# Spectral filter and FFN layers on one core: layer 1 folds along d by a half turn, with normalised rows and a constant table

## The chip, the cores and the metric

The kernel runs on 1 core of one Trainium2 chip. The metric is the time of one execution in device microseconds; lower is better. The engines are PE (TensorE matmul; PEld is its weight load), DVE (VectorE), ACT (ScalarE), POOL (GpSimd) and SP (SyncE, which here only issues DMAs).

## The reference

```python
def _A_ref(x, w_r, w_i):              # spectral filter over (S, D) = (2048, 448)
    X = jnp.fft.rfft2(x.astype(jnp.float32), axes=(-2, -1))
    X = X * (w_r + 1j * w_i)          # weights (2048, 225)
    return jnp.fft.irfft2(X, s=(S, D), axes=(-2, -1)).astype(jnp.bfloat16)

def _B_ref(x, w1, b1, w2, b2):        # FFN 448 -> 1792 -> 448
    h = jnp.einsum("bsd,df->bsf", x, w1) + b1
    r = jnp.where(h > 0, h, 0)
    return jnp.einsum("bsf,fd->bsd", r * r, w2) + b2

x = A_x                               # (1, 2048, 448) bf16
x = x + _A_ref(_layernorm(x), A_w_r, A_w_i)
x = x + _B_ref(_layernorm(x), B_w1, B_b1, B_w2, B_b2)
x = x + _A_ref(_layernorm(x), A_w_r, A_w_i)   # the same weights again
x = x + _B_ref(_layernorm(x), B_w1, B_b1, B_w2, B_b2)
```

## The kernel before

Two layers, each a spectral filter and an FFN. The 2048 rows lie in 16 tiles of 128 (row = 16 p + t), and stay on the chip. The Fourier transforms are matrix products.

A spectral stage of layer 1 runs through these steps; the names are those of the planner's tags.

- **A1** (`first_A`, one unit for each tile t): the transform of 128 points over the partitions. A tile of x is folded along d first: the table turns the sum and the difference of two halves of a row into even and odd parts. The folding happens on PE: the tile `xin` is multiplied by the table twice, and the second half of its row, mirrored, by the table with its signs. The mirrored half is a copy, `xr`, that lies in `VT` (`XR` items). The layer norm enters through the table: `Fs` is the constant table `FA_sb` (128x256) times the tile's 1/std, made anew for each tile, and a fifth matmul on `m2` (minus twice the mean) takes the mean away. So a tile has 5 matmuls of 256 columns; the last tile does them in two halves. The statistics come from DVE (`bn_stats`, `bn_aggr`), for tiles 1, 3 and 5 from two passes of ACT (`act_stats`); the root is ACT's, the reciprocal DVE's. The result is evacuated into `XA`.
- **TD** (`stage_TD`): the transform along d, 64 matmuls on `TD_sb`, evacuated into `arena`.
- **B**: 66 matmuls on `G_sb`, in four row and column groups of PE, again into `arena`.
- **W** (`stage_W`): 16 products on DVE with the filter weights `Wt`, into `wide`. `Wt` is filled by four gathers of 0.92 MB (indirect DMAs, issued by POOL, which need the index load `ix`). Each product reads from all four, so the first one waits for all.
- **Bi**: 256 matmuls on `H_sb`, in 8 blocks of 32, evacuated into `VT`.
- **TI, AI**: the inverse transform along d and over the partitions; TI needs all of `VT`. Then follow the second layer norm, the FFN (`W1_sb` and `W2_sb`, in the profile `W_sb`), and at the end of layer 1 the first transform of layer 2 (A2).

Every instruction is recorded by helpers (`mm`, `evac`, `scaled`, `act` and others) as an item. A planner gave the order of items on each engine, and this order is written out as tables of numbers, one for each engine (`ORDER`). At build time the items are placed in that order, waits on semaphores are derived from reads and writes, and fillers (matmuls on `ones`, line 1367) go into holes of PE that the planner's model sees, at the start and at two or three places later. DMAs go through the queues of SP, ACT (five of the loads of x) and POOL (the gathers); each queue works in its order, and a DMA behind a wait of its engine's sequencer is issued after that wait.

Some loads are gated by an `after`: the two halves of `H_sb` wait for the 1/std of tiles 10 and 12, `W1_sb` for the evacuation of Bi's block 1.

Of the kernel before, what the change touches and what calls it, by code (L numbers as in the profile page):

```python
# [150 lines left out]
1265 1270 1275 1236 1242 1280 1283 1286 1289 1292""",  # L151
    "act": """
# [11 lines left out]
1226 1035 1172 1184 1177 1174 1179 1182 1253 1246 1248 1251 1256 1261 1268 1278 1266 1263 1271 1258 1273 1276""",  # L164
    "dve": """
# [22 lines left out]
1039 1284 1281 1243 1287 1290 1293""",  # L188
    "pool": """
16 24 25 17 41 23 27 29 81 26 28 22 30 104 21 31 20 32 143 146 18 19""",  # L190
    "sp": """
3 5 6 8 9 11 13 15 33 34 35 150 151 152 153 154 155 156 157 158 159 233 234 235 236 281 301 319 322 321 339 357 375
# [1266 lines left out]
```

## Time and profile before

| | |
|---|---|
| median of 3 runs | 256.01 us (255.53 to 256.25) |
| the profiled execution, its own time | 255.97 us |
| its span | 254.2 us |
| PE busy | 246.8 us (97%), 2462 matmuls |
| DVE busy | 193.3 us (76%) |
| ACT busy | 166.4 us (65%) |
| POOL busy | 12.5 us (5%), all in the first 19 us |
| granted PE clock | 1.0 |

Times of the rows below are microseconds from the start of the span, and the 1.8 us between span and time are the same in every comparison made here. A row has start, length, engine, line, operation, out<-in, the shape, and in brackets how long the engine stood idle ahead of it and what released it. Instructions overlap a little, so a row of several is a better price for one than a row of one. A busy PE need not be at its peak.

### The profile page before, as it was taken

How to read it: one execution, taken by the hardware profiler on the slowest of the kernel's cores; microseconds unless marked ns; L12 is line 12 of the kernel's file. 1: busy time of each engine (PE TensorE's matmuls, PEld its weight loads, DVE VectorE, ACT ScalarE, POOL GpSimd, SP SyncE). 2: the span in 40 equal slices, each digit the busy share in tenths (PEclk: the TensorE clock that was granted, in tenths of full speed). 3: DMA queues.
4: the chain of work that ended last, by engine and by line, in shares of the span. 5: the costliest groups of instructions: out<-in, count | busy, mean ns of one | idle time of the engine just before them, and what ended most of it. 6: DMA issues, size and time to landing. Idle time of an engine off the chain costs nothing.

```text
span 254.2 us, 6150 instructions
## 1 busy us (share of the span) xinstructions
PE 246.8 (97%) x2462; PEld 154.2 (61%) x2462; DVE 193.3 (76%) x628; ACT 166.4 (65%) x362; POOL 12.5 (5%) x26
## 2 busy tenths in 40 slices
...
GB/s 198 367 330 383 56 148 327 96 41 45 36 41 44 0 4 0 41 43 3 0 3 1 3 3 3 3 44 43 59 81 23 0 3 41 38 87 64 3 0 146
DMA packets 24080, 18.10 MB, mean 71 GB/s; under 512 B 16082, under 2 KB 22706, under 8 KB 24052
## 3 DMA queue, kind: packets, MB, share of 16 engines
...
q10 hardware_dynamic: 720, 0.80, 1.1%
q8 instruction: 19, 0.31, 0.5%
q14 instruction: 9, 0.07, 0.1%
...
## 4 chain that ended last, share of the span: by engine, by line
PE 74%; DVE 10%; ACT 8%; DMA 4%; POOL 1%; issue 1%; SPq 0%; POOLq 0%; DVEq 0%
PE ps L724 74%; ACT arena L749 5%; DVE wide L778 3%; ACT VT L749 2%; DMA FA_sb<-c_FA 2%; DMA wide<-wide 2%; DVE st L854 1%; ACT wide L749 1%; DVE Fs L761 1%; DVE VT L750 1%; DVE XA L750 1%; DVE x_sb L1217 1%; POOL VT L750 1%; DVE arena L750 1%; PE ps L1367 0%
## 5 line engine op out<-in xcount | busy, mean ns | idle before, releaser
L724 PE MATMUL ps<-wide,W_sb 64*128 64x512 bf16 (+1 forms) x770 | 90.0, 346 | 0.2 <-DMA wide<-wide 0.2
L724 PE MATMUL ps<-W_sb,arena 128*128 128x448 bf16 (+3 forms) x476 | 86.8, 342 | 0.0
L724 PEld LDWEIGHTS ps<-wide,W_sb 64*128 64x128 bf16 (+1 forms) x770 | 51.4, 95 | 36.3 <-issue 0.7
L743 ACT ACTIVATE arena<-ps,b1col 128x512 bf16<-128x512 f32 x84 | 52.0, 691 | 29.2 <-PE ps L724 28.9
L724 PEld LDWEIGHTS ps<-W_sb,arena 128*128 128x128 bf16 x476 | 45.5, 98 | 38.1 <-ACT arena L743 0.4
L778 DVE TENSOR_TENSOR arena<-arena 128x512 bf16<-128x512 bf16 (+1 forms) x140 | 44.0, 362 | 29.8 <-ACT arena L743 29.8
L1095 ACT ACTIVATE VT<-x_sb 128x448 bf16<-128x448 bf16 x28 | 16.1, 582 | 13.2 <-DVE x_sb L1071 13.2
L749 ACT ACTIVATE arena<-ps 128x896 bf16<-128x896 f32 (+1 forms) x27 | 20.6, 852 | 3.1 <-PE ps L724 3.1
L743 ACT ACTIVATE mv<-mv,epst 128x1 f32<-128x1 f32 (+1 forms) x45 | 12.8, 297 | 12.0 <-DVE mv L855 8.4
L743 ACT ACTIVATE arena<-ps 128x256 bf16<-128x256 f32 x56 | 17.9, 400 | 0.9 <-PE ps L724 0.7
L778 DVE TENSOR_TENSOR wide<-arena,Wt 128x896 bf16<-128x896 bf16 x32 | 17.8, 620 | 0.4 <-ACT arena L749 0.4
L749 ACT ACTIVATE XA<-ps 128x512 bf16<-128x512 f32 (+1 forms) x28 | 15.3, 595 | 3.2 <-PE ps L724 3.2
L1217 DVE SCALAR_TENSOR_TENSOR x_sb<-ps,mv,xin 128x448 bf16<-128x448 f32 (+2 forms) x13 | 8.0, 644 | 11.7 <-PE ps L724 11.5
L724 PE MATMUL ps<-wide,VT 64*128 64x512 bf16 x42 | 15.8, 376 | 0.0
L749 ACT ACTIVATE wide<-ps 128x896 bf16<-128x896 f32 (+3 forms) x20 | 14.1, 762 | 2.4 <-PE ps L724 2.3
L724 PE MATMUL ps<-H_sb,wide 64*128 64x128 bf16 x512 | 15.5, 216 | 0.1
L724 PEld LDWEIGHTS ps<-H_sb,wide 64*128 64x128 bf16 x512 | 14.4, 94 | 2.0 <-ACT arena L749 1.3
L749 ACT ACTIVATE VT<-ps 128x512 bf16<-128x512 f32 (+1 forms) x16 | 12.2, 885 | 0.0
L1367 PE MATMUL ps<-ones 128*128 128x512 bf16 (+2 forms) x32 | 10.4, 450 | 1.7 <-POOL ones L791 1.0
L760 ACT ACTIVATE wide<-x_sb,rstd 128x448 bf16<-128x448 bf16 x12 | 7.8, 665 | 6.3 <-DVE mv L787 6.0
L750 DVE CAST arena<-ps 128x448 bf16<-128x448 f32 (+1 forms) x11 | 8.8, 831 | 3.1 <-PE ps L724 3.1
L1071 DVE SCALAR_TENSOR_TENSOR x_sb<-ps,mv,xin 128x448 bf16<-128x448 f32 x16 | 10.3, 677 | 0.8 <-PE ps L724 0.7
...
## 6 DMA issues: line engine op xcount, KB each, us to landing
...
xin<-in_A_x_dram SPq DMA_DIRECT2D x3, 224.0 KB
...
xin<-in_A_x_dram ACTq DMA_DIRECT2D x2, 224.0 KB, 5.0
...
```

The costliest lines, as they stand in the source:

```text
L724: return sch.add("pe", lambda e: e.matmul(_res(o), lhsT, rhs, start=start, stop=stop, skip_group_check=skip), [lhsT, rhs], [o], cost=cost, ...
L743: sch.add("act", lambda e: e.activation(o, _res(i), func, **kw), rd, [o], cost=c)
L749: op = sch.add(engs[0], lambda e: e.activation(o, _res(i), ACT.Copy) if h[0].eng == "act" else e.tensor_copy(o, _res(i)), [i], [o], cost=c ...
L750: e.tensor_copy(o, _res(i)), [i], [o], cost=c[engs[0]], unit=unit)
L760: op = sch.add(engs[0], lambda e: e.activation(o, i, ACT.Copy, scale=s) if h[0].eng == "act" else e.tensor_scalar(o, i, s, 1.0, op0=ALU.mu ...
L761: e.tensor_scalar(o, i, s, 1.0, op0=ALU.mult, op1=ALU.mult), [i, s], [o], cost=c[engs[0]])
L778: sch.add(eng, lambda e: e.tensor_tensor(o, _res(a), b, op), [a, b], [o], cost=_free(o) / rate + 69.0)
L854: small(lambda e, si=si, xi=xi: e.bn_stats(si, xi), [xi], [si], _free(xi) / 0.96 + 69.0)
L1071: small(lambda e, xx=xx, xi=xi, r=r, m=m: e.scalar_tensor_tensor(out=xx, in0=_res(r), scalar=m, in1=xi, op0=ALU.subtract, op1=ALU.add), [r ...
L1095: op = sch.add("act", lambda e, i=i, o=o, x=x, h=h: e.activation(o, x, ACT.Square, accum_out=sd[:, i, 1:2]) if h[0].eng == "act" else e.sc ...
L1217: small(lambda e: e.scalar_tensor_tensor(out=o, in0=_res(i), scalar=rs[0] if rs else 1.0, in1=xi, op0=ALU.add if t >= 4 and last else ALU. ...
L1367: return lambda e: e.matmul(ps[:, b, 0:n], ones[:], ones[:, None, :].to_broadcast([P, n // P, P]), start=True, stop=True)
```

## The change

The two halves of a row are now folded by a half turn (element d with d + 224) in place of a mirror image (d with 447 - d). The second half of the row can then be read where it lies, so the mirrored copies (`XR`, 9 items on POOL) go. The rows themselves are normalised into `xs`, which lies in `VT`: (x - mean) / std of a whole tile, 448 elements, on POOL or DVE (`normal`) or, for tiles 1, 3, 5 and 9, on ACT with a scale and a bias that DVE prepares. The first transform's table is then the constant `FA_sb`; the 16 scaled tables `Fs`, the items that make minus twice the mean, and the fifth matmul go. Tile 3 gets its statistics from DVE instead of ACT. `TD_sb` takes even and odd frequencies in two groups, and TD's evacuation puts them in order again, as layer 2's did before. The gate of H becomes the evacuation of tile 12 into `XA`, the gate of `W1_sb` the evacuation of Bi's block 3. The planner's model of DMA times is changed (with landing times of the loads given as a table), and all of `ORDER` is made anew.

```diff
-    l = np.arange(1, 225)[None, :]
-    th = 2 * np.pi * l * (dd - 223.5) / D
     TD = np.zeros((2, 2, P, LW))
-    for g, M in enumerate((np.cos(th), -np.sin(th))):
+    for g in range(2):
+        th = 2 * np.pi * np.arange(2 - g, 226 - g, 2)[None, :] * (dd - 223.5) / D
+        M = np.concatenate([np.cos(th), -np.sin(th)], 1)
...
     "pool": """
-16 24 25 17 41 23 27 29 81 26 28 22 30 104 21 31 20 32 143 146 18 19""",
+16 17 31 22 20 90 61 23 81 78 106 103 118 127 130 19 18 21""",
...
-ACT_STATS = (1, 3, 5)
+ACT_STATS = (1, 5)
+XN_ACT = (1, 3, 5, 9)
+GATE = 3
+HGATE = 12
...
-        xr = VT[:].rearrange("p a b t c -> p (a b t c)")[:, 0:NT * HD].rearrange("p (t d) -> p t d", t=NT)
+        xs = VT[:].rearrange("p a b t c -> p (a b t c)")[:, 0:NT * D].rearrange("p (t d) -> p t d", t=NT)
...
+        def normal(o, i, m, s, engs):
...
+            op = sch.add(engs[0], lambda e: e.tensor_scalar(o, i, m, s, op0=ALU.subtract, op1=ALU.mult), [i, m, s], [o],
+                         cost=c[engs[0]])
...
-                evac(xr[:, b:b + n, :], xin[:, b:b + n, D - 1:HD - 1:-1], EV["XR"])
...
         def first_A(t):
 
-            f = Fs[:, t % NFS, :]
-            scaled(f, FA_sb[:], rstd[:, t, 0:1], EV["FS"])
+            if t in XN_ACT:
+                nb = mv[:, t, 2:3]
+                small(lambda e: e.scalar_tensor_tensor(out=nb, in0=mv[:, t, 0:1], scalar=-1.0, in1=rstd[:, t, 0:1], op0=ALU.mult,
+                                                       op1=ALU.mult), [mv[:, t, 0:1], rstd[:, t, 0:1]], [nb])
+                act(xs[:, t, :], xin[:, t, :], ACT.Identity, bias=nb, scale=rstd[:, t, 0:1])
+            else:
+                normal(xs[:, t, :], xin[:, t, :], mv[:, t, 0:1], rstd[:, t, 0:1], EV["XN1"])
...
                 for k in range(2):
-                    mm(o(k), xin[:, t, D0[k]:D0[k] + P], F2, k == 0, False, skip=True, unit=u)
-                    mm(o(k), xr[:, t, D0[k]:D0[k] + P], F1, False, False, skip=True, unit=u)
-                mm(q[lambda b: ps[:, b, 0:4 * w].rearrange("p (k g c) -> p k g c", k=2, g=2)[:, :, 0, :]],
-                   m2[:, t, 0:1].to_broadcast([P, P]), F2, False, True, skip=True, unit=u)
+                    mm(o(k), xs[:, t, D0[k]:D0[k] + P], F2, k == 0, False, skip=True, unit=u)
+                    mm(o(k), xs[:, t, HD + D0[k]:HD + D0[k] + P], F1, False, k == 1, skip=True, unit=u)
...
                         if first:
-                            l0, w, m = g * LW, LW, TD_sb[:, g, k, :]
+                            r, m = 1 - g, TD_sb[:, g, k, :].rearrange("p (q i) -> p q i", q=2)
+                            o = t[lambda b, i=i, r=r: ps[:, b + i, :].rearrange("p (q w) -> p q w", q=2)[:, :, r * QD:(r + 1) * QD]]
...
-            dma("sp", H_sb[:, 8 * i:8 * i + 8], dc["H"][:, 8 * i:8 * i + 8], after=[rstd[:, 10 + 2 * i, 0:1]])
+            dma("sp", H_sb[:, 8 * i:8 * i + 8], dc["H"][:, 8 * i:8 * i + 8], after=[XA[:, 0, 0, 0, HGATE, :]])
...
-            after=[VT[:, :, :, NT - 1, 16:32]])
+            after=[VT[:, :, :, :, 0:1] if GATE is None else VT[:, :, :, NT - 1, 16 * GATE:16 * GATE + 16]])
```

What stands on POOL in the first transform before, from the first scaled table on (`Fs` the tables, `VT<-xin` the mirrored copies, `Wt` the gathers):

```order
L761 TENSOR_SCALAR Fs<-FA_sb,rstd 128x256
L827 DMA Wt<-in_A_w_i_dram,ix 128x3600
...
L827 DMA Wt<-in_A_w_r_dram,ix 128x3600
L750 COPY VT<-xin 128x448
L761 TENSOR_SCALAR Fs<-FA_sb,rstd 128x256
L827 DMA Wt<-in_A_w_i_dram,ix 128x3600
L750 COPY VT<-xin 128x448
L827 DMA Wt<-in_A_w_r_dram,ix 128x3600
L750 COPY VT<-xin 128x448
L761 TENSOR_SCALAR Fs<-FA_sb,rstd 128x256 x2
L791 MEMSET x_sb 128x4x32
```

And now (`VT<-xin,mv,rstd` is the normalisation of a tile into `xs`):

```order
L783 TENSOR_SCALAR VT<-xin,mv,rstd 128x448
L850 DMA Wt<-in_A_w_r_dram,ix 128x3600 x2
L783 TENSOR_SCALAR VT<-xin,mv,rstd 128x448 x2
L850 DMA Wt<-in_A_w_i_dram,ix 128x3600
L783 TENSOR_SCALAR VT<-xin,mv,rstd 128x448 x7
L814 MEMSET wide 128x16x16
L814 MEMSET x_sb 128x4x32
L850 DMA Wt<-in_A_w_i_dram,ix 128x3600
```

The second gather comes before the second tile, and the fourth moves behind all normalisations and both clears.

PE before, from TD to the end of Bi in layer 1 (`TD_sb`, `G_sb`, `H_sb` are the tables of TD, B and Bi):

```order
L724 MATMUL ps<-TD_sb,XA 128x224 x40
L724 MATMUL ps<-arena,G_sb 64x448 x3
L724 MATMUL ps<-arena,G_sb 64x224
L724 MATMUL ps<-arena,G_sb 64x448 x3
L724 MATMUL ps<-arena,G_sb 64x224 x3
L724 MATMUL ps<-arena,G_sb 64x448 x24
L724 MATMUL ps<-TD_sb,XA 128x224 x24
L724 MATMUL ps<-arena,G_sb 64x448 x24
L724 MATMUL ps<-H_sb,wide 128x2x16x4 x64
L724 MATMUL ps<-arena,G_sb 64x448 x8
L724 MATMUL ps<-H_sb,wide 128x2x16x4 x192
```

And now, at the same place:

```order
L737 MATMUL ps<-TD_sb,XA 128x2x112 x44
L737 MATMUL ps<-arena,G_sb 64x448 x16
L737 MATMUL ps<-TD_sb,XA 128x2x112 x12
L737 MATMUL ps<-arena,G_sb 64x448 x16
L737 MATMUL ps<-H_sb,wide 128x2x16x4 x32
L737 MATMUL ps<-arena,G_sb 64x448 x19
L737 MATMUL ps<-arena,G_sb 64x224
L737 MATMUL ps<-arena,G_sb 64x448 x3
L737 MATMUL ps<-arena,G_sb 64x224 x3
L737 MATMUL ps<-TD_sb,XA 128x2x112 x8
L737 MATMUL ps<-H_sb,wide 128x2x16x4 x64
```

The first block of Bi, which needs two products of W, moves ahead of 26 matmuls of B and the last 8 of TD; before, all of TD and all but 8 of B stood ahead of it.

ACT's start before, and now (the loads of x on its queue, the table load, the statistics of tile 1):

```order
L716 DMA xin<-in_A_x_dram 128x448 x2
L716 DMA xin<-in_A_x_dram 128x896
L716 DMA xin<-in_A_x_dram 128x448
L743 ACT_TABLE_LOAD
L743 ACTIVATE warm<-warm 128x1
L716 DMA xin<-in_A_x_dram 128x896
L876 ACTIVATE wide,mv<-xin 128x448 x2
```

```order
L756 ACT_TABLE_LOAD
L756 ACTIVATE warm<-warm 128x1
L729 DMA xin<-in_A_x_dram 128x448 x2
L729 DMA xin<-in_A_x_dram 128x896
L729 DMA xin<-in_A_x_dram 128x448
L884 ACTIVATE wide,mv<-xin 128x448
L756 ACTIVATE mv<-mv,epst 128x1
```

The table load moves ahead of the loads; the load of tiles 12 and 13, third row of two tiles before, now stands behind the normalisation of tile 1.

More of the change, by code (lines that the diff above doesn't have):

```diff
@@ L141 @@
     "pe": """
[9 rows of a table removed]
[L151 to L152 removed]
[11 rows of a table removed]
[L164 to L165 removed]
[22 rows of a table removed]
[L188 removed]
[9 rows of a table added]
+1249 1254 1259 1220 1226 1264 1267 1270 1273 1276""",
+    "act": """
[11 rows of a table added]
+1163 1035 1166 1168 1230 1232 1235 1242 1240 1247 1245 1237 1257 1260 1262 1250 1255 1252""",
+    "dve": """
[21 rows of a table added]
+1261 1246 1258 1238 1236 1263 1251 1248 1241 1256 1243 1253 1265 1268 1221 1227 1171 1271 1274 1277""",
     "pool": """
[L190 removed]
+16 17 31 22 20 90 61 23 81 78 106 103 118 127 130 19 18 21""",
     "sp": """
[L192 to L194 removed]
+8 9 10 11 12 13 14 15 24 25 26 134 135 136 137 138 139 140 141 142 143 217 218 219 220 265 285 303 306 305 323 341
+359 377 927 948 966 968 969 1125 986 1128 1131 1004 1134 1022 1219 1225 1175 1040 1178 1181 1172 1222 1269 1266 1228
+1272 1275 1278""",
 }
@@ L197 @@
 LOOK = {}
[L198 removed]
+EV = {'A1': ['act', 'dve'], 'A2': ['act'], 'TD': ['act', 'dve'], 'B': ['act', 'dve'], 'Bi': ['act', 'dve'], 'TI': ['act'], 'TI1': ['act', 'dve'], 'M': ['act', 'dve'], 'T': ['act', 'dve'], 'XN1': ['pool', 'dve'], 'FS2': ['dve'], 'XN': ['act', 'dve']}
 PAIRS = (2, 4, 6, 8, 10, 12, 14)
@@ L203 @@
 A1GROUPS = ((0, 1), (1, 1), (2, 1), (3, 1), (4, 1), (5, 1), (6, 2), (8, 2), (10, 2), (12, 2), (14, 2))
-ACT_STATS = (1, 3, 5)
+ACT_STATS = (1, 5)
 HALVES = True
+XN_ACT = (1, 3, 5, 9)
+GATE = 3
+HGATE = 12
+LANDS = {"L.xin.448": 3450.0, "L.xin.2240": 4040.0, "L.xin.3584": 6500.0, "L.xin.1344": 7100.0, "L.xin.5376": 9600.0, "L.xin.0": 3270.0, "L.xin.896": 3770.0, "L.FA_sb.0": 6350.0, "L.xin.1792": 6900.0, "L.ix.0": 7500.0, "L.xin.2688": 8100.0, "L.xin.4480": 8700.0, "L.xin.6272": 9300.0, "L.TD_sb.0": 9900.0, "L.G_sb.0": 11200.0, "L.G0_sb.0": 11450.0}
+XLOADS = ((1, 1, "act"), (5, 1, "act"), (8, 2, "act"), (3, 1, "act"), (12, 2, "act"), (0, 1, "sp"), (2, 1, "sp"), (0, 0, "sp"), (4, 1, "sp"), (1, 0, "sp"), (6, 2, "sp"), (10, 2, "sp"), (14, 2, "sp"))
 LATE = (4, 4)
@@ L298 @@
     NDSEM = {"sp": 40, "pool": 8, "act": 5, "pe": 0, "dve": 0}
-    DMA_FIRST = 3500.0
+    DMA_FIRST = 2000.0
+    LAND = 400.0
+    LANDS = LANDS
     TURN = 100.0
@@ L438, in ready_of @@
                             same = d.eng == u.eng and not d.is_dma
-                            r = max(r, done[d] + d.lat + (40.0 if u.eng == "pe" else 0.0) - off)
+                            r = max(r, done[d] + (60.0 if d.is_dma and d.cost != 1000.0 else d.lat) + (40.0 if u.eng == "pe" else 0.0) - off)
                     off += op.cost
@@ L565, in schedule @@
                 if op.is_dma:
-                    dma_free = max(dma_free, t + 1800.0) + op.lat
-                    done[op] = dma_free
+                    if op.cost == 1000.0:
+                        dma_free = done[op] = max(dma_free, t + 1800.0) + op.lat
+                    else:
+                        begin = max(dma_free, t + (450.0 if e == "pool" else 1100.0))
+                        land = self.LANDS.get(u.tag)
+                        if land is None:
+                            dma_free = begin + op.lat * (1.1 if begin < 3400.0 else 1.8 if begin < 5000.0 else 1.08)
+                            done[op] = dma_free + (400.0 if begin < 3800.0 else 1200.0 if begin < 6500.0 else 900.0 if begin < 9000.0 else 500.0)
+                        else:
+                            done[op], dma_free = land, max(dma_free, land - 400.0)
                 for w in op.takes:
@@ L764, in scaled @@
                 op.alt = {e: c[e] for e in engs}
+        def normal(o, i, m, s, engs):
+            n = _free(o)
+            c = {"dve": n / 1.92 + 69.0 + 100.0, "pool": 0.83 * n + 245.0}
+            h = []
+            op = sch.add(engs[0], lambda e: e.tensor_scalar(o, i, m, s, op0=ALU.subtract, op1=ALU.mult), [i, m, s], [o],
+                         cost=c[engs[0]])
+            h.append(op)
+            if len(engs) > 1:
+                op.alt = {e: c[e] for e in engs}
         def affine(o, i, s, b, engs):
@@ L809, in bass_interleave_layers__spectral_gfnet__dense_activation_squared_relu__prompt_kernel @@
         sch.table_deps = [sch.last_write[k] for k in _pages(warm[:, 0:1])][:1]
-        for a, n, q in ((0, 1, "sp"), (1, 1, "act"), (2, 1, "sp"), (3, 1, "act"), (4, 1, "sp"), (5, 1, "act"), (6, 2, "sp"),
-                        (8, 2, "act"), (10, 2, "sp"), (12, 2, "act"), (14, 2, "sp")):
-            dma(q, xin[:, a:a + n, :], x_dram[:, a:a + n, :])
-            if a == 2:
-                dma("sp", FA_sb[:], dc["FA"])
-            if a == 4:
-                dma("sp", ix[:], dc["ix"])
+        for a, n, q in XLOADS:
+            if n:
+                dma(q, xin[:, a:a + n, :], x_dram[:, a:a + n, :])
+            elif a:
+                dma(q, ix[:], dc["ix"])
+            else:
+                dma(q, FA_sb[:], dc["FA"])
         memset(ones[:], 1.0, eng="pool")
@@ L827, in gather @@
             sch.add("pool", lambda e: e.indirect_dma_start(o, None, (A_w_r, A_w_i)[w], bass.IndirectOffsetOnAxis(ix[:, c:c + 1], 0)),
-                    [ix[:, c:c + 1]], [o], is_dma=True, cost=1150.0, lat=160.0 * n)
+                    [ix[:, c:c + 1]], [o], is_dma=True, cost=1150.0, lat=138.0 * n)
         sch.bias, sch.tag = PR["M"], "M"
@@ L835, in bass_interleave_layers__spectral_gfnet__dense_activation_squared_relu__prompt_kernel @@
             gather(1, w, WS * (2 + w), 16)
-        for a in range(0, NT, 2):
-            for b in range(a, a + 2) if a == 0 else (a,):
-                n = 1 if a == 0 else 2
-                sch.bias, sch.tag = PR["A1"] - PR["A1step"] * a / 2, f"XR.{b}"
-                evac(xr[:, b:b + n, :], xin[:, b:b + n, D - 1:HD - 1:-1], EV["XR"])
         sch.bias, sch.tag = 0.0, ""
@@ L857, in ln_stats @@
             act(mu[:, a:b, 1], mu[:, a:b, 1], ACT.Sqrt, bias=epst[:, 0:1])
-            if mean:
-                twice_mean(a, b)
-            else:
+            if not mean:
                 ts(mu[:, a:b, 2], mu[:, a:b, 0], 4.0, 1.0, ALU.mult, ALU.mult)
-        def twice_mean(a, b):
-            m, i = m2[:, a:b, 0], mv[:, a:b, 0:1].to_broadcast([P, b - a, 2])
-            def twice(e):
-                with nc.allow_low_precision(reason="two equal terms"):
-                    return e.tensor_reduce(m, i, mybir.AxisListType.X, ALU.add, negate=True)
-            small(twice, [mv[:, a:b, 0]], [m])
         def act_stats(t):
```

29 lines of the change are left out of this document (11 added, 18 removed), and 83 rows, old and new, of the table ORDER.

## Prediction

> **What bounds the kernel now.** I read the busy table by stages first, then the chain that ended last, then the timelines of PE, POOL, DVE and ACT up to 44 us, last the DMA landings. Rows of the busy table (stretch, length, busy time and instructions of PE, PEld, DVE, ACT, POOL, then clock, DMA share, GB/s):
>
> ```profile
> 0.00:19.72 19.72, 16.49 (x106) 9.76 (x106) 14.56 (x61) 15.83 (x42) 12.54 (x26) 1.00 0.87 302
> 19.72:38.10 18.38, 17.85 (x388) 14.99 (x389) 15.47 (x24) 15.79 (x23) 0.00 (x0) 1.00 0.57 188
> ```
>
> The first row is the first transform, the second the rest of the first spectral layer. The clock is 1.00 in both. The chain (start, length, what):
>
> ```profile
> 17.46 2.12 DVE XA L750 x4
> ...
> 19.72 4.01 PE ps L724 x40
> ...
> 38.12 5.66 PE ps L724 x74
> ...
> 43.82 90.13 PE ps L724 x689
> ```
>
> From 38.12 on PE hardly waits, so a microsecond won or lost ahead of 38.12 reaches the end one for one. Before 19.72 POOL and DVE set the pace. Between them lies a stage in which PE looks full:
>
> ```profile
> 19.72 3.99 PE L724 MATMUL ps<-TD_sb,XA 128*128 128x224 bf16 x40 [0.35 <-DVE XA L750]
> ...
> 25.29 2.47 PE L724 MATMUL ps<-TD_sb,XA 128*128 128x224 bf16 x24
> 27.69 1.33 PE L724 MATMUL ps<-arena,G_sb 64*64 64x448 bf16 x24
> ...
> 31.36 5.68 PE L724 MATMUL ps<-H_sb,wide 64*128 64x128 bf16 x192
> 36.97 0.60 PE L1367 MATMUL ps<-ones 128*128 128x512 bf16 x2
> 38.12 1.32 PE L724 MATMUL ps<-TI_sb,VT 112*128 112x224 bf16 x16 [0.55 <-DVE VT L750]
> ```
>
> From 19.72 to 36.97 PE has 17.25 us of work without a hole, and 1.15 us later the inverse transform (TI) starts. A gain of the first transform passes to the end if PE stays fed in these 17 us. That hangs on the filter multiplications on DVE, which need all four gathers of the weights:
>
> ```profile
> 24.92 0.63 DVE L778 TENSOR_TENSOR wide<-arena,Wt 128x896 bf16<-128x896 bf16 x1
> ...
> 28.03 7.08 DVE L778 TENSOR_TENSOR wide<-arena,Wt 128x896 bf16<-128x896 bf16 x13
> ```
>
> The first is at 24.92; 13 take 7.08, so 0.53 each with overlap.
>
> **The change: the first transform.** On PE it takes the mean matmuls of 16 tiles away, 256 columns each. A TD matmul of 224 columns takes 0.10, so these are some 1.8 us; but PE waits for operands there (16.49 busy of 19.72, fillers on `ones` included), so they are worth nothing by themselves. What counts is who makes the operands. Before, POOL copies 9 mirrored blocks and scales 5 tables; after, it normalises 10 tiles of 448. POOL's rows:
>
> ```profile
> 3.21 0.69 POOL L750 COPY VT<-xin 128x224 bf16<-128x224 bf16 x2 [2.28 <-DMA xin<-in_A_x_dram]
> ...
> 7.91 1.15 POOL L827 DMA_INDIRECT Wt<-in_A_w_i_dram,ix  x1 [0.93 <-DMA ix<-c_ix]
> 9.08 1.06 POOL L750 COPY VT<-xin 128x448 bf16<-128x448 bf16 x2
> ...
> 13.99 1.03 POOL L827 DMA_INDIRECT Wt<-in_A_w_i_dram,ix  x1 [0.17 <-issue]
> ...
> 15.76 0.97 POOL L827 DMA_INDIRECT Wt<-in_A_w_r_dram,ix  x1 [0.17 <-PE ps L724]
> ...
> 17.56 0.94 POOL L761 TENSOR_SCALAR Fs<-FA_sb,rstd 128x256 bf16<-128x256 bf16 x2 [0.26 <-DVE rstd L885]
> ...
> 18.59 0.31 POOL L791 MEMSET wide<- 128x256 f32 x1
> ```
>
> A POOL normalisation of 448 is not in this trace. Lower bound: a copy of that size, 0.53. Upper: the scaling of 256 takes 0.47; all of it per element gives 0.47 x 448/256 = 0.82. Copies of 224 and 448 (0.35, 0.53) differ by 0.8 ns an element, and 0.47 + 192 x 0.83 ns = 0.63, which I take.
>
> POOL in its new order: two gathers from 7.91 (the index load does not move) to 10.0; two normalisations to 11.3; a gather to 12.3; seven normalisations, 4.4 us, to 16.7; two clears, 0.4 (18.50 to 18.90 before), to 17.1; the last gather is issued there, at about 17.2, 1.4 us later than before. Before, the last scaling ended at 18.50 and the next stage (TD) began 1.22 later, after the matmuls and evacuations of the last tile. The same tail after 16.7 gives 17.9.
>
> DVE must keep pace:
>
> ```profile
> 14.49 0.62 DVE L854 BATCH_NORM_STATS2 st<-xin 128x6 f32<-128x448 bf16 x1
> ...
> 16.48 0.27 DVE L761 TENSOR_SCALAR Fs<-FA_sb,rstd 128x256 bf16<-128x256 bf16 x1
> 16.67 0.22 DVE L868 TENSOR_REDUCE m<-mv 128x2 bf16<-128x4 f32 x2
> 16.80 0.58 DVE L761 TENSOR_SCALAR Fs<-FA_sb,rstd 128x256 bf16<-128x256 bf16 x1
> ```
>
> It loses 7 table scalings (0.2 to 0.5 of the queue each, some 2.4) and 11 mean reductions (0.07 each, 0.8), and gains one statistic (0.54), two normalisations (0.3 to 0.6 each) and four small products (0.3): about 1.5 us less. With 12 statistics after 6.6 it ends its list at about 15.4, ahead of POOL. The scaling at 16.80 lasts 0.58 instead of 0.27 and ends when POOL's copy, from 16.72 on, ends. The Trainium skill's page "SBUF — State Buffer" (Two separate sides) says that the two share a port pair, which the first to start holds for its whole instruction; the row agrees, and by it either normalisation on DVE may cost up to one of POOL's.
>
> ACT drops one tile's two statistics passes and four table scalings and gains four normalisations:
>
> ```profile
> 2.62 1.28 ACT L743 ACT_TABLE_LOAD   x1 [2.62 <-issue]
> 2.69 0.39 ACTq L716 DMA_DIRECT2D xin<-in_A_x_dram  x1
> ...
> 4.03 0.56 ACT L876 ACTIVATE wide<-xin 128x448 bf16<-128x448 bf16 x1
> ...
> 5.14 0.28 ACT L743 ACTIVATE mv<-mv,epst 128x1 f32<-128x1 f32 x1
> 5.33 0.65 ACT L877 ACTIVATE wide<-xin,mv 128x448 bf16<-128x448 bf16 x1
> ...
> L760 ACT ACTIVATE wide<-x_sb,rstd 128x448 bf16<-128x448 bf16 x12 | 7.8, 665 | 6.3 <-DVE mv L787 6.0
> ...
> xin<-in_A_x_dram ACTq DMA_DIRECT2D x2, 224.0 KB, 5.0
> ```
>
> Its table load now stands ahead of the loads it issues. The DMA at 2.69 went out while the table load ran, so the loads lose some 0.2 us, and ACT can begin at about 3.6 instead of 4.03. From there: passes of two tiles (0.56 and 0.65) 2.4, 11 roots of 0.19 (5.14 to 5.33) 2.1, four normalisations (a scaling of that size takes 0.67, some 0.1 of it overlapped) 2.3, 13 evacuations at DVE's 0.53 each 6.9. That is 13.7, so not before 17.3; with two or three short waits 17.9, as late as POOL. The load of tiles 12 and 13 now stands behind a wait on this queue (about 5.8 instead of 2.69). Loads of that size landed in 5.0, so by 10.9, and DVE reaches them at about 12. No cost; if they came after 12.2, ACT and POOL would be late next. TD starts at 18.0: **1.7 us gained.**
>
> **The change: what gives it back.** The gathers and the table H, issue rows and time to landing:
>
> ```profile
> 16.44 0.80 SPq L716 DMA_DIRECT2D H_sb<-c_H  x2
> ...
> Wt<-in_A_w_i_dram,ix POOLq DMA_INDIRECT x1, 5.1
> Wt<-in_A_w_r_dram,ix POOLq DMA_INDIRECT x1, 9.0
> ...
> 18.70:24.10 5.40, 5.05 (x66) 4.73 (x67) 3.05 (x4) 3.17 (x6) 0.20 (x1) 1.00 1.02 390
> ```
>
> The third gather landed at 13.99 + 5.1 = 19.1. The last, beside H, landed at 15.76 + 9.0 = 24.76, 5.7 later; the first multiplication followed at 24.92. So the gathers set that start already. H is now gated by an evacuation of tile 12 on DVE, about 16.7 against 16.44. The last gather, issued at 17.2, meets all of H again. Alone it would land at 17.2 + 5.1 = 22.3. With its share of 390 GB/s halved, its 0.92 MB need 2.4 more: 24.7. If its bytes start 2.7 after issue (5.1 less 2.4) and take the 5.7 of before: 25.6. I take 25.3, nearer to the last, since that is the same pair of transfers; with POOL's two prices the ends are 21.4 (22.3 less 9 x 0.1) and 27.3 (25.6 and 9 x 0.19).
>
> From the first multiplication to TI it is 13.2 us before. After, PE stands at the first Bi block until two multiplications are done (1.15), and then has 256 H matmuls (192 in 5.6: 7.5), 33 G (0.05 each: 1.7), 8 TD (0.8) and the 1.15 to TI: 12.3. DVE has 16 multiplications (8.5) and five evacuations between them, and ends close behind PE; I add 0.1. TI: 25.3 + 12.4 = **37.7 against 38.12: 0.4 gained.** PE alone would allow 18.0 + 17.25 + 1.15 = 36.4.
>
> TD keeps its columns, but its evacuation now reads in strides of 112, as layer 2's does already. ACT's evacuations into the arena in layer 1 and in layer 2 (min, median, max in ns):
>
> ```profile
> L749 ACT ACTIVATE arena<-ps x14: 537/917/1011, 21.4 to 32.1; 128x896 bf16<-128x896 f32 x10, 128x448 bf16<-128x448 f32 x4
> ...
> L749 ACT ACTIVATE arena<-ps x13: 538/923/967, 140.0 to 150.8; 128x896 bf16<-128x896 f32 x11, 128x448 bf16<-128x448 f32 x2
> ```
>
> The medians are equal, so I take nothing, 0 to 0.1. W1's load waits for block 3 instead of block 1, in the new order about 4 us before TI, so near 34:
>
> ```profile
> 34.04 1.00 SPq L716 DMA_DIRECT2D W_sb<-in_B_w_dram  x2
> ...
> 44.02 2.14 PE L724 MATMUL ps<-wide,W_sb 128*128 128x256 bf16 x18
> ```
>
> It was issued at 34.04 and used at 44.02; it stays hidden as long as it lands by 43. The rest of the program has the same instructions in an order that differs by a few places, and SP now stores between transposes; PE is full there, so 0, with 0.3 either way.
>
> **Sum.** The profiled execution took 255.97 (span 254.2 and 1.8 around it); the median is 256.01. 255.97 - 1.7 + 1.3 = 255.6.
>
> **Rivals.** (1) The gather comes in time. If it lands by 24.0, PE never stands and all 1.7 pass: 254.3. For it: 5.1 us for the gather at 13.99, and H would be partly through. Against it: 9.0 for the one beside H. The Trainium skill's page "DMA: Bandwidth & Descriptors" (Anatomy of one DMA) gives 2.0 us plus bytes at 436 GB/s; for 0.92 MB that is 4.1, by which it would land at 21.3, an estimate, and this rival would be the outcome; the rows of 5.1 and 9.0 are both above it. (2) POOL is the new bound. At 0.82 a normalisation the nine ahead of the last gather cost 1.7 more: TD at about 19.6, gather issued at 18.9, landing near 27.0, TI at 39.4: 257.2, slower. It decides from a landing of 26.5 on, that is from 0.76 a normalisation. For it: 0.47 for only 256. Against: the small slope of the copies. (3) The change doesn't shorten the first transform: ACT, with 13.7 us of work in 14.3, waits for DVE's statistics, TD stays near 19.5 and TI near 38.1: 256.0. The near full ACT speaks for it, DVE's 1.5 us against.
>
> **How the numbers follow.** The forecast has 0.42, its own range 255.0 to 256.3; rival 1 has 0.34, rival 2 0.15, rival 3 0.09. Before is measured to about 0.3% (0.77 us): faster means under 255.24. Faster: 0.34 and 0.05 from the forecast's end, 0.39. Slower: 0.15 and 0.02 of later stalls, 0.17. Same: 0.44. The range 254.2 to 257.0 holds the forecast, most of rival 1 and half of rival 2.
>
> **What would show it.** TD's first matmul at 17.5 to 18.5; POOL normalisations of 0.6 to 0.7; the last gather issued near 17.2 and landing 24.7 to 25.6; DVE idle for 2 us or more before its first multiplication; PE's hole before the first H matmul; TI between 37.1 and 38.3. The forecast is wrong if that gather lands before 24 or after 26.5, or if a stall after 44 us passes 0.5 us.

## The result, and the profile after

The changed kernel takes 268.52 us (median; 268.34 to 270.27), the kernel before 256.13 in the same session: a ratio of 1.0499 [1.0462, 1.0536], 12.4 us slower. The forecast was 255.6 with a range to 257.0. The profiled execution took 268.44 (span 266.7).

The busy table over the same two stretches as before (columns as there):

```profile
0.00:19.72 19.72, 12.55 (x62) 5.90 (x63) 11.34 (x47) 13.50 (x34) 13.94 (x15) 0.99 0.81 274
19.72:38.10 18.38, 14.56 (x113) 9.75 (x115) 6.80 (x9) 6.25 (x10) 10.36 (x8) 0.73 0.50 166
```

In the second stretch, where PE, DVE and ACT had 15 us and more of work and POOL none, POOL is now busy for 10.4 us, DVE and ACT for less than 7, and PE's granted clock is 0.73. The page gives the clock in 40 slices, and POOL's costliest group (busy, mean ns of one):

```profile
PEclk9995799999999999999999999999999999999999
...
L783 POOL TENSOR_SCALAR VT<-xin,mv,rstd 128x448 bf16<-128x448 bf16 x10 | 18.6, 1863 | 4.6 <-DVE rstd L892 4.0
```

A POOL normalisation takes 1.86 us; I had taken 0.63. The chain that ended last now runs through POOL (start, length, what):

```profile
17.60 4.24 POOL VT L783 x3
21.84 1.29 issue
23.13 5.53 POOL VT L783 x3
28.66 0.25 POOL wide L814
29.22 8.20 DMA Wt<-in_A_w_i_dram,ix
37.61 1.70 DVE wide L801 x3
...
49.79 6.25 PE ps L737 x84
56.17 90.25 PE ps L737 x691
```

POOL's queue holds the last gather behind all ten normalisations. It goes out at 29.22, lands 8.2 us later, and the first filter multiplication follows at 37.61. PE's timeline has the first TD matmul in the same picture:

```profile
28.72 0.62 PE L737 MATMUL ps<-FA_sb,VT 128*128 128x128 bf16 x8 [1.23 <-POOL VT L783]
29.17 0.38 PE L1374 MATMUL ps<-ones 128*128 128x512 bf16 x1
29.72 5.97 PE L737 MATMUL ps<-TD_sb,XA 128*128 128x224 bf16 x44 [0.17 <-DVE XA L763]
```

The stations side by side, in us from the span's start; the forecast's FFN start is its TI and the 5.90 that before took from TI to there, its end 255.6 less the 1.8 around the span:

| station | before | forecast | after |
|---|---|---|---|
| TD starts | 19.72 | 18.0 | 29.72 |
| last gather issued | 15.76 | 17.2 | 29.22 |
| last gather lands | 24.76 | 25.3 | 37.42 |
| first multiplication | 24.92 | 25.3 | 37.61 |
| TI starts | 38.12 | 37.7 | 49.79 |
| first FFN matmul on W1 | 44.02 | 43.6 | 56.17 |
| end of the span | 254.2 | 253.8 | 266.7 |

The first multiplication comes 12.7 us later than before, TI 11.7, the end 12.5: the loss lies ahead of that multiplication, one microsecond of it comes back up to TI, and 0.8 are lost again behind TI.

### The profile page after: what moved, and what is told of

Read it like the earlier page. It is cut to its first block, busy times and chain, and to the rows that moved or that the text cites. A ratio compares the mean times of both kernels' runs of the same rounds, so it can differ in the third digit from the quotient of the medians.

```text
span 266.7 us, 6101 instructions
## 1 busy us (share of the span) xinstructions
PE 250.9 (94%) x2449; PEld 160.3 (60%) x2449; DVE 193.8 (73%) x618; ACT 165.8 (62%) x358; POOL 24.3 (9%) x22
## 3 DMA queue, kind: packets, MB, share of 16 engines
HBM read 12.20 MB, written 1.84 MB: 53 GB/s over the span
## 4 chain that ended last, share of the span: by engine, by line
PE 72%; ACT 9%; DVE 6%; POOL 6%; DMA 4%; issue 1%; DVEq 0%; POOLq 0%
PE ps L737 72%; POOL VT L783 6%; ACT arena L762 4%; DVE wide L801 3%; DMA Wt<-in_A_w_i_dram,ix 3%; ACT VT L762 2%; ACT wide L762 1%; DMA xin<-in_A_x_dram 1%; ACT XA L762 1%; ACT mv L756 1%; DVE VT L763 1%; DVE arena L763 1%; PE ps L1374 0%; DVE rstd L892 0%; DVE st L872 0%
## 5 line engine op out<-in xcount | busy, mean ns | idle before, releaser
L737 PEld LDWEIGHTS ps<-wide,W_sb 64*128 64x128 bf16 (+1 forms) x770 | 56.7, 95 | 30.4 <-issue 1.7
L801 DVE TENSOR_TENSOR arena<-arena 128x512 bf16<-128x512 bf16 (+1 forms) x140 | 45.8, 366 | 30.7 <-ACT arena L756 30.1
L762 ACT ACTIVATE arena<-ps 128x896 bf16<-128x896 f32 (+1 forms) x26 | 19.8, 856 | 5.4 <-PE ps L737 5.4
L1102 ACT ACTIVATE VT<-x_sb 128x448 bf16<-128x448 bf16 x28 | 16.1, 575 | 10.4 <-DVE x_sb L1078 10.4
L737 PE MATMUL ps<-FA_sb,VT 128*128 128x256 bf16 (+1 forms) x68 | 11.0, 310 | 9.0 <-POOL VT L783 8.6
L783 POOL TENSOR_SCALAR VT<-xin,mv,rstd 128x448 bf16<-128x448 bf16 x10 | 18.6, 1863 | 4.6 <-DVE rstd L892 4.0
L1224 DVE SCALAR_TENSOR_TENSOR x_sb<-ps,mv,xin 128x448 bf16<-128x448 f32 (+2 forms) x13 | 8.1, 645 | 10.4 <-PE ps L737 10.3
L737 PEld LDWEIGHTS ps<-FA_sb,VT 128*128 128x128 bf16 x68 | 6.2, 109 | 14.3 <-POOL VT L783 12.4
L756 ACT ACTIVATE mv<-mv,epst 128x1 f32<-128x1 f32 (+1 forms) x45 | 12.5, 295 | 2.8 <-DVE mv L873 2.7
L1374 PE MATMUL ps<-ones 128*128 128x512 bf16 (+1 forms) x36 | 11.6, 448 | 2.6 <-POOL ones L814 1.0
L763 DVE CAST arena<-ps 128x896 bf16<-128x896 f32 (+1 forms) x12 | 9.9, 853 | 5.1 <-PE ps L737 5.1
```

Source lines behind the costliest of these rows:

```text
L737: return sch.add("pe", lambda e: e.matmul(_res(o), lhsT, rhs, start=start, stop=stop, skip_group_check=skip), [lhsT, rhs], [o], cost=cost, ...
L756: sch.add("act", lambda e: e.activation(o, _res(i), func, **kw), rd, [o], cost=c)
L762: op = sch.add(engs[0], lambda e: e.activation(o, _res(i), ACT.Copy) if h[0].eng == "act" else e.tensor_copy(o, _res(i)), [i], [o], cost=c ...
L763: e.tensor_copy(o, _res(i)), [i], [o], cost=c[engs[0]], unit=unit)
L783: op = sch.add(engs[0], lambda e: e.tensor_scalar(o, i, m, s, op0=ALU.subtract, op1=ALU.mult), [i, m, s], [o], cost=c[engs[0]])
L801: sch.add(eng, lambda e: e.tensor_tensor(o, _res(a), b, op), [a, b], [o], cost=_free(o) / rate + 69.0)
```

## The experiments

Three questions: why does a POOL normalisation cost three times its estimate, is that all of the loss, and what would be left without it?

**POOL's prices.** One kernel times seven forms on POOL with the other engines idle:

```
e.tensor_copy(o, i)
e.tensor_scalar(o, i, 1.5, 1.0, mult, mult)
e.tensor_scalar(o, i, p, 1.0, mult, mult)
e.tensor_scalar(o, i, p, 1.5, subtract, mult)
e.tensor_scalar(o, i, p, r, mult, mult)      # and mult, add
e.tensor_scalar(o, i, p, r, subtract, mult)
```

> A kernel of its own: POOL alone works on rows of x, seven forms of a two-step elementwise instruction at 128, 256 and 448 elements, three each, with DVE idle; the output is x, so nothing of the reference is computed. Theory A (the second scalar read from memory is what makes POOL slow): the forms with one scalar from memory and one constant take about 0.63 us at 448 and 0.47 at 256; those with two scalars from memory take about 1.85 at 448 and 1.1 at 256, whatever the operations. Theory B (subtract is slow): the slow ones are the two with subtract, also with a single scalar from memory. Theory C (the place or the length of the operands in the changed kernel, or DVE beside it): all forms at 448 take about 0.63 here.

Its groups, by form and size (busy, mean ns of one):

```profile
L125 POOL TENSOR_SCALAR y_ptr_ptr_sub_mult<-xin,par 128x448 bf16<-128x448 bf16 x3 | 5.6, 1917 | 0.0
L98 POOL TENSOR_SCALAR y_ptr_imm_sub_mult<-xin,par 128x448 bf16<-128x448 bf16 x3 | 5.3, 1803 | 0.0
...
L119 POOL TENSOR_SCALAR y_ptr_ptr_sub_mult<-xin,par 128x128 bf16<-128x128 bf16 x3 | 2.4, 841 | 0.0
L116 POOL TENSOR_SCALAR y_ptr_ptr_mult_add<-xin,par 128x448 bf16<-128x448 bf16 x3 | 2.2, 759 | 0.0
L107 POOL TENSOR_SCALAR y_ptr_ptr_mult_mult<-xin,par 128x448 bf16<-128x448 bf16 x3 | 2.1, 747 | 0.0
...
L89 POOL TENSOR_SCALAR y_ptr_imm_mult_mult<-xin,par 128x448 bf16<-128x448 bf16 x3 | 1.9, 651 | 0.0
...
L71 POOL COPY y_copy<-xin 128x448 bf16<-128x448 bf16 x3 | 1.6, 563 | 0.0
...
L110 POOL TENSOR_SCALAR y_ptr_ptr_mult_add<-xin,par 128x128 bf16<-128x128 bf16 x3 | 1.3, 482 | 0.0
...
L65 POOL COPY y_copy<-xin 128x128 bf16<-128x128 bf16 x3 | 0.8, 293 | 7.9 <-DMA xin<-in_A_x_dram 7.9
```

The form of the changed kernel takes 1.92 us with nothing else running, so neither DVE nor the loads make it slow. A second factor from memory adds 0.1 (0.65 to 0.75). The subtract adds 1.15, and it grows with size: (1917 - 841) / 320 = 3.4 ns an element, against (759 - 482) / 320 = 0.87 for mult and add and 0.84 for the copy.

The second table asks which forms with a subtract are slow:

```
e.tensor_scalar(o, i, p, None, subtract)      # alone
e.tensor_scalar(o, i, 1.5, 1.0, subtract, mult)   # and add, mult
e.tensor_scalar(o, i, p, r, add, mult)        # and mult, subtract
e.tensor_scalar(o, i, 0.0, 1.0, max, mult)
e.tensor_tensor(o, i, i2, mult)               # and add, subtract
```

> A second price table of POOL instructions alone (the kernel copies x to its output and does nothing else of the computation), at 128 and 448 columns, three of each. The first table gave 0.65 us for (mult by a pointer, mult) at 448 columns, 0.76 for (mult, add) with two pointers, and 1.80 for (subtract, mult). Theory S, it is the subtract operation itself: every form with a subtract takes 1.7 to 1.9 us at 448 (subtract alone, subtract of a constant, mult then subtract, and the two-input subtract as against the two-input add), every form without it 0.55 to 0.8 (add then mult 0.76; the two-input ones perhaps 0.7 to 1.0). Theory F, only the operation in the first place of the scalar form is slow unless it is a mult: add then mult and max then mult take 1.8 too, and mult then subtract 0.76.

```profile
L89 POOL TENSOR_SCALAR y_ptr_mult_sub<-xin,par 128x448 bf16<-128x448 bf16 x3 | 5.6, 1902 | 0.0
L95 POOL TENSOR_SCALAR y_max_imm<-xin 128x448 bf16<-128x448 bf16 x3 | 5.1, 1752 | 0.0
...
L65 POOL TENSOR_SCALAR y_sub_only<-xin,par 128x448 bf16<-128x448 bf16 x3 | 4.2, 1409 | 0.0
L113 POOL TENSOR_TENSOR y_tt_sub<-xin 128x448 bf16<-128x448 bf16 x3 | 3.1, 1091 | 0.0
L107 POOL TENSOR_TENSOR y_tt_add<-xin 128x448 bf16<-128x448 bf16 x3 | 3.1, 1088 | 0.0
...
L83 POOL TENSOR_SCALAR y_ptr_add_mult<-xin,par 128x448 bf16<-128x448 bf16 x3 | 2.1, 747 | 0.0
...
L77 POOL TENSOR_SCALAR y_add_imm<-xin 128x448 bf16<-128x448 bf16 x3 | 1.6, 582 | 0.0
```

Neither theory holds as written. A scalar form is slow with a subtract in either place, but max is slow too, and the two-input subtract costs what the two-input add costs (1.09). What the rows show: scalar forms of mult and add alone, in any order and from constants or pointers, take 0.57 to 0.76, and those with a subtract or a max 1.4 to 1.9.

**A second factor from memory, in place.** The kernel before, with the second factor of POOL's five table scalings read from memory:

```diff
-e.tensor_scalar(o, i, s, 1.0, op0=ALU.mult, op1=ALU.mult)
+e.tensor_scalar(o, i, s, warm[:, 0:1] if h[0].eng == "pool" else 1.0, op0=ALU.mult, op1=ALU.mult)
```

> The kernel before, where the second factor of POOL's 5 table scalings (the constant 1.0) is read from memory instead (a 1.0 that lies there); nothing else changes. Theory A: these scalings of 256 elements go from 0.47 to about 1.1 us; the two at the end of the first transform stand one behind the other, so TD starts 1.2 to 2 us later: 257.3 to 258. Theory B or C: 0.47 each and 256.0 us.

257.39 us, ratio 1.0053 [1.0024, 1.0082]. A scaling takes 0.55 to 0.56 instead of 0.47, which bears out the table. The time lies where Theory A put it, but not for its reason: its scalings were to take 1.1, and TD starts only 0.33 later (20.05). The last gather went out 0.27 us later than before (16.03), yet landed 2.3 later:

```profile
H_sb<-c_H SPq DMA_DIRECT2D x1, 768.0 KB, 10.5
Wt<-in_A_w_r_dram,ix POOLq DMA_INDIRECT x1, 11.0
```

DVE waited 1.9 us for it, and TI came at 39.77 instead of 38.12. The landing of that gather, 9.0 us after its issue before and 11.0 here, is the looser number of the two.

**Without the subtract.** The changed kernel, with POOL only multiplying by 1/std, so that the mean stays in its ten tiles:

```diff
-e.tensor_scalar(o, i, m, s, op0=ALU.subtract, op1=ALU.mult)
+e.tensor_scalar(o, i, s, 1.0, op0=ALU.mult, op1=ALU.mult) if h[0].eng == "pool" else e.tensor_scalar(o, i, m, s, op0=ALU.subtract, op1=ALU.mult)
```

> The changed kernel, with POOL's 10 tiles only multiplied by 1/std (a constant 1.0 as the second factor); the mean stays in these rows, where each table of a nonzero frequency sums to zero over a constant, so the result is the reference's up to rounding. Theories A and B: POOL takes 0.63 each, and the rest of the prediction's sum can be read: TD starts near 18.0, the last gather is issued near 17.2 and lands near 25.3, TI near 37.7, 255.6 us. Theory C: still 1.85 each, about 268.5 us. Rival on the rest of the sum: the gather lands by 24 and the time is 254.3.

260.84 us, ratio 1.0194 [1.0165, 1.0224]: 7.7 of the 12.4 us are back. This is the kernel that the forecast priced, 0.62 a normalisation, and it still missed 255.6 by 5. TD starts at 18.20 (forecast 18.0). PE then stands for the last gather:

```profile
18.20 4.38 PE L737 MATMUL ps<-TD_sb,XA 128*128 128x224 bf16 x44 [0.17 <-DVE XA L763]
...
28.70 0.38 PE L737 MATMUL ps<-arena,G_sb 64*64 64x448 bf16 x2 [3.11 <-DVE wide L801]
29.01 1.37 PE L737 MATMUL ps<-H_sb,wide 64*128 64x128 bf16 x32
30.31 2.46 PE L737 MATMUL ps<-arena,G_sb 64*64 64x448 bf16 x26
...
41.70 1.71 PE L737 MATMUL ps<-TI_sb,VT 112*128 112x112 bf16 x24 [0.41 <-ACT VT L762]
```

The gather went out at 17.69 and landed 10.1 us later, at 27.8. Behind the hole of 3.1 us the granted clock is low (column after the five engines):

```profile
29.00:41.70 12.70, 12.29 (x303) 9.71 (x302) 11.38 (x20) 11.03 (x15) 0.00 (x0) 0.87 0.19 53
```

0.13 x 12.7 = 1.65 us. In the trace's clock record it is 0.50 from 29.61 to 33.03, 3.4 us, and 1.00 on either side. The 26 G matmuls take 2.46 there; in the run with the gather early, below, they take 1.33.

**The same tiles on VectorE.** The ten normalisations leave POOL's list and stand in VectorE's, each behind its 1/std:

```diff
-    "pool": 16 17 31 22 20 90 61 23 81 78 106 103 118 127 130 19 18 21
+    "pool": 16 17 22 20 23 19 18 21
```

> The changed kernel with POOL's 10 normalisations moved to DVE (0.37 us each there), each right behind the reciprocal that it needs; POOL then has only clears and gathers. If POOL's normalisations are the whole loss: DVE's list ends about 3 us later than in the changed kernel (17.2), TD starts near 19, all gathers are issued by 12.5 and landed by 20, PE has no hole before the first H matmul, TI at 19 + 17.25 + 1.15 = 37.4, 255.3 us. If the new order of the rest or the lower clock costs by itself: 258 us or more.

257.99 us, ratio 1.0071 [1.0046, 1.0096], 2.7 above the first theory and where the other one begins. All gathers are out by 12.7, PE has no hole, the clock is 1.00, and from TD to TI it is 18.49 us against 18.40 before; the new order by itself costs only the 0.8 us behind TI that the next section takes up. But TD starts at 21.04, 2 us later than expected and 2.8 later than in the scale-only kernel. DVE's list ends late: two normalisations take 0.70, so ten are 3.5 us, and DVE was nearly full already (14.5 us of the first 19.72 busy in the scale-only kernel). I had counted about 3 us for them, to an end at 17.2; the list ends at about 18.8 here and at 15.7 in the scale-only kernel.

```profile
18.15 0.70 DVE L762 TENSOR_SCALAR VT<-xin,mv,rstd 128x448 bf16<-128x448 bf16 x2
18.77 2.21 DVE L742 CAST XA<-ps 128x512 bf16<-128x512 f32 x4
```

**The subtract rewritten.** POOL computes x / std + (-mean / std); DVE makes -mean / std in seven more small instructions:

```diff
-e.tensor_scalar(o, i, m, s, op0=ALU.subtract, op1=ALU.mult)
+e.tensor_scalar(xs[:, t, :], xin[:, t, :], rstd[:, t, 0:1], mv[:, t, 2:3], op0=ALU.mult, op1=ALU.add)
```

> The changed kernel with POOL's ten normalisations as x * (1/std) + (-mean/std), a mult and an add instead of a subtract and a mult; -mean/std is seven more small VectorE instructions. Nothing else moves. If the subtract alone made POOL late: a normalisation at 0.76 us (first table) instead of 1.86, so the ten take 7.6 us instead of 18.6; the first TD matmul at 18.20 (the scale-only kernel, 0.62 each) + about 1.0 to 1.3 = 19.2 to 19.5; the last gather issued at 18.8, landing 8 to 10 us later, 27 to 29; TI at 41.5 to 43; 260.5 to 262. Rival: VectorE's added small instructions delay it further, TD at 20 or later and 262.5 or more.

260.13 us, ratio 1.0152 [1.0094, 1.0211], a little under the 260.5 to 262 expected. The same arithmetic as the changed kernel's, 8.4 us faster. TD starts at 19.83, half a microsecond later than expected, since POOL waits four times for DVE; the last gather goes out at 19.31 and lands at 28.4, as expected. TI is at 41.06, not 41.5 to 43, because the hole ahead of H is short and the clock stays at 1.00:

```profile
27.16 0.60 PE L1361 MATMUL ps<-ones 128*128 128x512 bf16 x2
29.24 1.16 PE L717 MATMUL ps<-H_sb,wide 64*128 64x128 bf16 x32 [1.47 <-DVE wide L781]
```

**The last gather earlier.** In the kernel just shown and in the scale-only kernel, the last gather (21) is moved up, right behind the third (23); POOL's list of the scale-only kernel:

```diff
-    "pool": 16 17 31 22 20 90 61 23 81 78 106 103 118 127 130 19 18 21
+    "pool": 16 17 31 22 20 90 61 23 21 81 78 106 103 118 127 130 19 18
```

> The scale-only kernel (POOL multiplies by 1/std and leaves the mean in; all else as changed) with the last gather issued right behind the third on POOL. Theory H: no hole, clock 1.0, TD at 18.2 + 1.0 = 19.2, TI at 37.6, 255.4, against 260.84 with the gather last. Theory Q: over 258.

256.60 us, ratio 1.0007 [0.9981, 1.0033]. Theory H holds: TD at 19.18 (19.2 expected), no hole, clock 1.00, TI at 37.66 (37.6):

```profile
19.18 4.38 PE L737 MATMUL ps<-TD_sb,XA 128*128 128x224 bf16 x44 [0.18 <-DVE XA L763]
...
26.50 1.07 PE L737 MATMUL ps<-H_sb,wide 64*128 64x128 bf16 x32
27.50 1.33 PE L737 MATMUL ps<-arena,G_sb 64*64 64x448 bf16 x26
...
37.66 1.71 PE L737 MATMUL ps<-TI_sb,VT 112*128 112x112 bf16 x24 [0.42 <-ACT VT L762]
```

TI is 0.46 us earlier than in the kernel before, and so is, by 0.40, the first matmul on W2 (57.24 against 57.64). The first TD matmul of layer 2 comes 0.66 later (140.06 against 139.40), and the span ends 0.7 later. What the first layer's transform gained is lost at the passage to layer 2, which the next section takes up; that is why the ratio is 1.00 and not the 255.4 that I expected.

> The same with the last gather issued right behind the third on POOL, ahead of seven normalisations, instead of behind all of them. Theory H, what the scale-only kernel still lost is the hole on TensorE that waited for the last gather (3.1 us) and the lower granted clock behind it (0.87 over 12.7 us, 1.65 us): with the gather issued at about 12.4 it lands before 23, no hole, clock 1.0; the issue costs POOL about 1.0 us ahead of the normalisations, so TD at 20.2 to 20.5, TI 18.4 us later (the stretch of the kernel before, 19.72 to 38.12) at 38.7, 256.6. Theory Q, the gathers are late because the transfers share the engines with the tables and the H loads, not because of the issue: the last one still lands after 26 or pushes other loads (H) back as far, and the time stays over 259.

258.09 us, ratio 1.0077 [1.005, 1.0105], 1.5 above Theory H, and the hole is gone as it said. The trace is of an execution that took 259.60, itself 1.5 above this median. In it TD starts at 22.27 instead of 20.2 to 20.5; from there to TI it is 18.48 as expected. Its first matmuls were late and slow: the first 12 on the table take 2.62 us and end at 10.5, in the two kernels above 1.47 us and 8.4 to 8.7, and POOL then waited 2.56 us for DVE. The trace's clock record begins at 10.24, with 1.00; in the two others at 4.4 and 5.9. Why it was so, and where TD starts in the other executions, isn't shown.

```profile
7.91 2.62 PE L717 MATMUL ps<-FA_sb,VT 128*128 128x256 bf16 x12
```

**The clock.** Two kernels put filler matmuls into the gaps. In the scale-only kernel, 15 of them stand in the hole ahead of H (the planner is told a longer landing of the last gather, 6.4 us):

```diff
-cost=1150.0, lat=138.0 * n)
+cost=1150.0, lat=LASTLAT if (w, a) == (1, WS * 1) else 138.0 * n)
```

> The scale-only kernel with the last gather at POOL's end (260.84 us; POOL leaves the mean in), and 15 filler matmuls of 0.21 us on TensorE in the hole ahead of the first H matmul, where it stood 3.1 us for the last gather. Theory C: the hole stays (first H matmul at about 29.0, since the gather lands no earlier), but the granted clock behind it is 1.0 instead of 0.87 over 12.7 us: TI at 40.0 to 40.2 instead of 41.70, 259.2. Rival: the 1.65 us between first H and TI are other waits (VectorE's or ScalarE's), not the clock: TI at 41.5 or later and 260.5 or more.

259.22 us, ratio 1.0150 [1.0135, 1.0165], as expected from the clock, which is 1.00 throughout. The hole is as long as it was; only what stands in it changed, and from the first H matmul to TI it is 11.51 us instead of 12.69:

```profile
25.46 3.41 PE L1375 MATMUL ps<-ones 128*128 128x512 bf16 x15
28.80 1.07 PE L738 MATMUL ps<-H_sb,wide 64*128 64x128 bf16 x32
29.80 1.33 PE L738 MATMUL ps<-arena,G_sb 64*64 64x448 bf16 x26
...
40.31 1.72 PE L738 MATMUL ps<-TI_sb,VT 112*128 112x112 bf16 x24
```

In the changed kernel itself, with the subtract, the fillers stand between the groups of the first transform:

```diff
-c = {"dve": n / 1.92 + 69.0 + 100.0, "pool": 0.83 * n + 245.0}
+c = {"dve": n / 1.92 + 69.0 + 100.0, "pool": 1860.0}
```

> The changed kernel with the same order of work on VectorE, ScalarE, POOL and SP, but with filler matmuls on TensorE between the groups of the first transform that wait for POOL (the planner is told 1.86 us for a POOL normalisation, and lays fillers into the gaps that it then sees; it was told 0.62). Theory C: of the 12.4 us, 10.0 are the start of TD and 1.7 the lower granted clock behind the gaps (0.77 over 7.3 us in the changed kernel). With fillers the clock stays at 1.0: TD at 29.4 to 29.7, TI 18.4 us later instead of 20.1, at 47.9 to 48.1; 266.7 to 266.9 against 268.5. Rival: the clock does not hang on TensorE's idling there, or the fillers stand in the way of the matmuls behind them: clock below 0.99 or TD later than 29.9, and 268 or more.

268.46 us, ratio 1.0498 [1.0483, 1.0513]: nothing gained, though the clock is 1.00 in every stretch. My Theory C was right on the clock and fell on the time. TD starts at 30.12, 0.4 later than in the changed kernel, as POOL's list runs 0.5 later; it takes 4.39 us instead of 5.97, and then PE waits, because the last gather (out at 29.70, landing 7.8 later) lets the first multiplication begin at 37.66, as in the changed kernel at 37.61:

```profile
30.12 4.39 PE L737 MATMUL ps<-TD_sb,XA 128*128 128x224 bf16 x44
...
38.34 0.38 PE L737 MATMUL ps<-arena,G_sb 64*64 64x448 bf16 x2 [0.82 <-DVE wide L801]
38.65 1.07 PE L737 MATMUL ps<-H_sb,wide 64*128 64x128 bf16 x32
...
49.81 1.71 PE L737 MATMUL ps<-TI_sb,VT 112*128 112x112 bf16 x24 [0.27 <-DVE VT L763]
```

In the changed kernel the low clock lay beside the wait for that gather and cost nothing. It costs where it comes behind the wait, as in the scale-only kernel.

No version beat the kernel before. The nearest, the scale-only one with the early gather, equals it and leaves the mean in; of those that remove the mean, VectorE's (257.99) and the rewritten subtract with the gather early (258.09) come closest.

## Why the prediction was wrong

The step that failed is the price of a POOL normalisation. I bounded it by 0.53 and 0.82 and took 0.63; it measured 1.86. Both bounds came from rows of other operations, a copy and a multiplication, and the slope between them was right for those: the scale-only kernel ran at 0.62. The subtract was in the diff, and no row of the trace had one on POOL, so the upper bound was no bound. Nine normalisations stand between the first gather and the last: 9 x 1.23 = 11.1 us. Waits and gaps between POOL's instructions, 0.9 more, make the 12.0 by which the last gather went out late.

The rest of the miss of 12.8 us, by the terms of the sum:

- Landing of the last gather, 8.1 after its issue forecast: 8.2 measured. The size was right by luck: H, whose share I had charged for it, went out 3.4 us ahead of it (25.84) and not beside it. Where H did go beside it, it took 10.1 in the scale-only kernel and 11.0 in the kernel before with its scalings slowed. The ends that I gave the landing were 21.4 and 27.3; the 27.8 of the scale-only kernel lies above both. I had also read that the gathers set the first multiplication before. The profile shows no wait for them there: DVE's cast ends at 24.88, behind the landing at 24.76, so the landing had about 0.1 us to spare.
- First multiplication to TI, 12.4 forecast: 12.2 measured, and 12.7 in the scale-only kernel with fillers. Right.
- The first transform, TD at 18.0 with POOL at 0.63: 18.20 at 0.62. Right, and with it the prices of DVE and ACT behind it: 0.40 for a normalisation on DVE (the second one took 1.18 beside POOL's), 0.75 on ACT, a little above the 0.67 taken.
- The low clock was no term of mine. It cost nothing in the changed kernel (268.46 with fillers) and 1.0 to 1.6 us in the scale-only one (13.68 from the first multiplication to TI against 12.72 with fillers; 260.84 against 259.22, in two sessions).
- TI to the end, 0 with 0.3 either way: 216.9 us instead of 216.1, so 0.8 late and outside the range. The first FFN matmul follows TI by 6.38 us instead of 5.90 in every variant of the changed kernel, but this is only order: all 64 TI matmuls now stand ahead of it, 56 before. The first matmul on W2 follows TI by 19.59 against 19.52. The loss is at the passage to layer 2, from the last group on W2 (`W_sb,arena`) to layer 2's TD (`TQ_sb`), before and after:

```profile
134.67 1.50 PE L724 MATMUL ps<-W_sb,arena 128*128 128x224 bf16 x14
...
139.40 2.44 PE L724 MATMUL ps<-TQ_sb,XA 112*128 112x112 bf16 x44
```

```profile
146.24 1.50 PE L737 MATMUL ps<-W_sb,arena 128*128 128x224 bf16 x14
...
151.80 2.44 PE L737 MATMUL ps<-TQ_sb,XA 112*128 112x112 bf16 x44
```

That is 4.73 us before and 5.56 after, and 5.54 to 5.57 in every variant of the changed kernel. PE waits there for rows that DVE makes (0.37) and for an evacuation by DVE (0.31), against one wait of 0.22 before. I had taken PE to be full there; which place in the new order does it is not tested.

With the price right, the sum would still have missed. The scale-only kernel's 260.4 (profiled execution) is 255.6 and 0.5 for a later issue, 2.0 for the longer landing, 0.2 to the first multiplication, 1.3 from there to TI, most of it the clock, 0.8 behind TI.

Rival 2 had the mechanism (POOL as the bound, the last gather behind it) with 0.15; its price, 0.82 at most, gave it 257.2. Rival 1 fell in the other direction: issued beside H, the gather never took less than 9.0 us. By the Trainium skill's page "DMA: Bandwidth & Descriptors" (Anatomy of one DMA) it would have been 4.1, an estimate; the landings read here lie between 5.1 and 11.0. Rival 3 didn't arise: with POOL at 0.62, ACT let TD start at 18.20.

The Trainium skill's "GPSIMD Engine Reference" (Engine selection) says that one-input operations on this engine run at roughly line rate. The tables agree for a copy, mult and add (0.84 to 0.87 ns an element) and not for a subtract (3.4).

The Trainium skill's page "TensorE: Matmul & The Clock Gate" (Part 1: The HAM clock gate) says that the array falls to half rate after an idle window of about 3.4 us and comes back after as long a stretch of work. The scale-only run nearly agrees: a hole of 3.1 us, then 3.4 us at a clock of 0.50. The changed kernel doesn't agree on the idle window: its clock fell to 0.50 at 19.37 and at 29.61, and no hole in the ten microseconds ahead of either was longer than 1.84 us. PE was busy for 1.05 and 1.45 of the 3.41 us ahead of these two falls, and for 0.91 in the scale-only kernel. With the rewritten subtract, a hole of 1.47 us left the clock at 1.00; PE was busy for 1.93 of the 3.40 us from 27.20 on.
